# Batches of a K or V pair on separate partition halves, in a decode step of two attention and two GLU layers

## The chip, the cores and the metric

One NeuronCore of a Trainium2 chip runs the whole program. Times are device microseconds of an execution, as medians of repeated runs. PE is TensorE's matmul side, PEld its weight loads, DVE VectorE, ACT ScalarE, POOL GpSimd, SPq the queue from which the loads are issued. The profile counts sixteen DMA engines for the core, and before the change the loads fill 97.2% of their time.

## The reference

Four decode sequences of one token each go through attention, GLU, attention, GLU, each with a layer norm ahead and a residual add behind. Both attention layers use the same caches and weights, and so do both GLU layers.

```python
B, Sq, D, Hq, Hkv, Sk, Dh = 4, 1, 512, 32, 8, 8192, 128     # bf16
W = min(4096, max(256, Sk // 4))                            # window: 2048
q = (x @ wq).reshape(B, Sq, Hq, Dh).transpose(0, 2, 1, 3)
k = repeat(k_cache[:, :, Sk - W:, :], 4, axis=1)            # caches are [B, Hkv, Sk, Dh]
v = repeat(v_cache[:, :, Sk - W:, :], 4, axis=1)
p = softmax(einsum("bhqd,bhkd->bhqk", q, k) * Dh ** -0.5)
o = einsum("bhqk,bhkd->bhqd", p, v)                         # then @ wo
# GLU: (sigmoid(x @ w_gate) * (x @ w_up)) @ w_down, F = 1792
```

The windows of K and V hold 16 MiB each. K is read once and kept on the chip for the second attention layer; V is read nearly twice, 30 loads of 1 MiB, since the 25 MiB that the program sets aside (`arena`, below) do not take both whole.

## The kernel before

A small list scheduler lays out the operations of each engine from their dependencies; all loads stand in one order on the SP queue. `arena` holds 50 slots of 128 partitions x 2048 elements. A "pair" is a tile of two slots with the windows of two batches of one KV head: 2 x 512 KB = 1 MiB. One load brings it in.

```python
def pair_d(cache, h, bp):                        # the DRAM side of a K or V load
    return cache[2 * bp:2 * bp + 2, h, SK - W:SK, :].rearrange(
        "b (p j) d -> p b (j d)", p=64)          # 64 rows x 2 batches x 4096 elements

def load_k(h):
    where[("K", h)] = h
    for bp in range(2):
        dma("K%d_%d" % (h, bp), kpair(h, bp), pair_d(A_k, h, bp), w=tok(4 * h + 2 * bp), rate="bw_8k")
```

The SBUF side is a tile of 128 partitions x 4096 elements. Row p of batch b thus lands on partition 2p + b: the two batches of a pair lie interleaved over the partitions. A row is 32 tokens, 8 KB, contiguous in DRAM.

DVE transposes K (1219 ns for 128x1024 words, mean of 32 in the profile before). The program takes the result as blocks of 32 x 32 words of two bf16 elements, each transposed, so that a partition then holds some dimensions of many tokens. A score unit is 16 matmuls of 128x512, four for each of four column groups of PE. Their records overlap: 588 to 669 ns for one, and 2.00 us for the 16 of the unit at 134.49 us.

```python
for cp in range(4):
    for b in range(NB):
        gi = 2 * (b % 2) + b // 2
        kt = kpair(hk, b // 2).rearrange("p (j c x i t) -> p c t i j x", c=2, x=16, i=2, t=2)
        q0 = ((k2 * NB + b) * 4 + cp) * NR
        last = pe.matmul(ps[32 * gi:32 * gi + NR, bank, :], qbd[:, q0:q0 + NR],
                         kt[:, cp // 2, cp % 2, b % 2, :, :], start=(cp == 0), stop=(cp == 3))
```

The moving side takes x at a step of four elements (i and t lie between), because the two batches alternate. Softmax takes a row maximum on DVE and the exponential on ACT; P is then turned to stand ahead of P.V:

```python
for jh in range(2):
    for i in range(2):
        last = pe.matmul(ps[:, PBS[i], 0:256], perm[64 * i:64 * i + 64, jh * 128:(jh + 1) * 128],
                         prow[64 * i:64 * i + 64, jh * 256:(jh + 1) * 256], start=(jh == 0), stop=(jh == 1))
# ... one ACT eviction of 128x512, one DVE transpose, then 32 P.V matmuls for each pair
```

Of the kernel before, what the change touches and what calls it, by code (L numbers as in the profile page):

```python
# [6 lines left out]
F32 = mybir.dt.float32  # L7
BF16 = mybir.dt.bfloat16
ACTF = mybir.ActivationFunctionType
ALU = mybir.AluOpType  # L10
AXX = mybir.AxisListType.X
# [261 lines left out]
def build(nc, A_x, A_k, A_v, A_wq, A_wo, B_wg, B_wu, B_wd, out, cfg=None):  # L273
    cfg = dict(cfg or {})
    tm = dict(_TM)
# [8 lines left out]
    NB, SQ, D = A_x.shape  # L284
    _, HKV, SK, DH = A_k.shape
    HQ = A_wq.shape[1] // DH
    REP = HQ // HKV
    W = min(4096, max(256, SK // 4))
    NJ = W // 128
# [6 lines left out]
    NR = 4 * REP  # L296
# [18 lines left out]
    with es:  # L315
        def sb(name, shape, dt):
            return es.enter_context(nc.sbuf_tensor(name, shape, dt))

        arena = sb("arena", [128, NS * SLOT], BF16)
        prow = sb("prow", [128, 512], BF16)  # L320
        ebuf = sb("ebuf", [128, 512], F32)
        qbd = sb("qbd", [128, 2 * NB * 4 * NR], BF16)
        qh = sb("qh", [128, 2 * 64], BF16)
        qrep = sb("qrep", [128, 2 * 256], BF16)
        ones_f = sb("ones_f", [128, 32], F32)
        ident_b = sb("ident_b", [128, 128], BF16)
        perm = sb("perm", [128, 2 * 128], BF16)
        sel_f = sb("sel_f", [128, NR], F32)
        sel_b = sb("sel_b", [128, NR], BF16)
        s3 = sb("s3", [128, 2 * 3], BF16)  # L330
        sres = sb("sres", [128, 2], F32)
        sel_r = sb("sel_r", [128, REP], F32)
        maskr = sb("maskr", [128, 32], F32)
        mxt = sb("mxt", [128, 2 * 32], F32)
        nmax = sb("nmax", [128, 4], F32)
        psm = sb("psm", [128, 2], F32)
        rinv = sb("rinv", [128, 2 * NR], F32)
        onb = sb("onb", [128, 2 * NR], BF16)
# [9 lines left out]
        ps = es.enter_context(nc.psum_tensor("ps", [128, 8, 512], F32))  # L348
# [5 lines left out]
        P = _Plan()  # L354
# [3 lines left out]
        PBS = (2, 3)  # L358
# [17 lines left out]
        def c_act(n):  # L376
            return tm["act_fix"] + n * tm["act_el"]
# [43 lines left out]

        def pair_d(cache, h, bp):

            return cache[2 * bp:2 * bp + 2, h, SK - W:SK, :].rearrange("b (p j) d -> p b (j d)", p=64)

        def kpair(h, bp):
            return tile_ap(4 * h + 2 * bp)
# [81 lines left out]
        def load_v(h, bp, k, n_use):  # L509
# [6 lines left out]
                                       base=0, channel_multiplier=-1),  # L516
             r=[("ones_f",)], w=[("ident_b",)])
# [4 lines left out]

        for jh in range(2):
            for bp in range(2):
                P.op("gpsimd", "perm%d_%d" % (jh, bp), 300.0,
                     lambda g, jh=jh, bp=bp: g.affine_select(
                         perm[:, jh * 128:(jh + 1) * 128].rearrange("p (a x) -> p a x", a=4)[
                             :, :, 16 * jh + 8 * bp:16 * jh + 8 * bp + 8].rearrange("p a (i r) -> p a i r", i=2),
                         ones_f[:, :].rearrange("p (a i r) -> p a i r", a=4, i=2),
                         [[-REP, 4], [-64, 2], [-1, REP]], ALU.is_equal, 0.0,  # L530
                         base=-32 * bp, channel_multiplier=1),
                     r=[("ones_f",), ("perm",)], w=[("perm", jh, bp)])
        perms = [("perm", jh, bp) for jh in range(2) for bp in range(2)]
        P.op("vector", "sel_f", 200.0,
             lambda v: v.tensor_reduce(sel_f[:, :],
                                       perm[:, 0:128].rearrange("p (a x) -> p a x", a=4)[:, :, 0:NR].rearrange("p a x -> p x a"),
                                       AXX, ALU.add),
             r=perms, w=[("sel_f",)])
        P.op("gpsimd", "sel_b", 200.0, lambda g: g.tensor_copy(sel_b[:, :], sel_f[:, :]),
             r=[("sel_f",)], w=[("sel_b",)])  # L540
        P.op("vector", "sel_r", 100.0,
             lambda v: v.tensor_reduce(sel_r[:, :], sel_f[:, :].rearrange("p (g r) -> p r g", g=4), AXX, ALU.add),
             r=[("sel_f",)], w=[("sel_r",)])
        P.op("vector", "maskr", 100.0,
             lambda v: v.tensor_scalar(maskr[:, :].rearrange("p (y r) -> p y r", r=REP),
                                       sel_r[:, :].unsqueeze(1).broadcast_to([128, 8, REP]),
                                       1.0, 1.0e30, ALU.subtract, ALU.mult),
             r=[("sel_r",)], w=[("maskr",)])

        o = P.op("scalar", "x_in", 1300.0, lambda e: e.dma_start(x_nat, x_d), w=[("prow",)])  # L550
        o.sem = ("xin",)
# [108 lines left out]
        def q_unit(tag, h, k2):  # L660

            for a in range(4):
                dst = qbd[32 * a:32 * a + 32, k2 * 256:(k2 + 1) * 256].rearrange(
                    "p (x y) -> p x y", y=NR)[:, :, a * REP:(a + 1) * REP]
                src = qrep[32 * a:32 * a + 32, h * 64:(h + 1) * 64].rearrange("p (x r) -> p x r", r=REP)
                rd = [("qrep", h // 4)]
                if a % 2 == 0:
                    P.op("vector", "qe%s_%d" % (tag, a), c_dve(64), lambda v, dst=dst, src=src: v.tensor_copy(dst, src),  # L668
                         r=rd, w=[("q", k2, a)])
                else:  # L670
                    P.op("scalar", "qe%s_%d" % (tag, a), c_act(64), lambda s_, dst=dst, src=src: s_.copy(dst, src),  # L671
                         r=rd, w=[("q", k2, a)])
# [10 lines left out]
        def softmax_unit(tag, hk):  # L683
            u = ucount[0]
            ucount[0] += 1
            k2 = u % 2
            bank = SB[k2]
            q_unit(tag, hk, k2)

            def e_s(pe):  # L690
                last = None
                for cp in range(4):
                    for b in range(NB):
                        gi = 2 * (b % 2) + b // 2
                        kt = kpair(hk, b // 2).rearrange("p (j c x i t) -> p c t i j x", c=2, x=16, i=2, t=2)
                        q0 = ((k2 * NB + b) * 4 + cp) * NR
                        last = pe.matmul(ps[32 * gi:32 * gi + NR, bank, :], qbd[:, q0:q0 + NR],  # L697
                                         kt[:, cp // 2, cp % 2, b % 2, :, :], start=(cp == 0), stop=(cp == 3))
                return last
            P.op("tensor", "S" + tag, 16 * tm["pe_row"], e_s,  # L700
                 r=[("slot", 4 * hk + t) for t in range(4)] + [("q", k2, a) for a in range(4)],
                 w=[("pss", k2)], banks=(bank,))
            mk = mxt[:, k2 * 32:(k2 + 1) * 32]
            P.op("vector", "mx" + tag, c_dve(512),
                 lambda v: v.tensor_reduce(nmax[:, k2:k2 + 1], ps[:, bank, :], AXX, ALU.max),  # L705
                 r=[("pss", k2)], w=[("mx", k2)], banks=(bank,))
            P.op("vector", "mk" + tag, tm["dve_small"],
                 lambda v: v.tensor_scalar(mk, maskr[:, :], nmax[:, k2:k2 + 1], None, ALU.add),
                 r=[("mx", k2), ("maskr",)], w=[("mk", k2)])
            P.op("vector", "nm" + tag, tm["dve_small"],  # L710
                 lambda v: v.tensor_reduce(nmax[:, 2 + k2:3 + k2], mk, AXX, ALU.max, negate=True, apply_transpose=True),  # L711
                 r=[("mk", k2)], w=[("nm", k2)])
            P.op("scalar", "ex" + tag, c_act(512) + 200.0,
                 lambda a: a.activation(prow[:, :].rearrange("p (m x t) -> p m x t", x=16, t=2),  # L714
                                        ps[:, bank, :].rearrange("p (m t x) -> p m x t", x=16, t=2), ACTF.Exp, bias=nmax[:, 2 + k2:3 + k2], scale=1.0,
                                        accum_out=psm[:, k2:k2 + 1]),
                 r=[("pss", k2)] + [("nm", k2)], w=[("prow",), ("psm", k2)], banks=(bank,))
            return k2

        def turn_p(tag, k2):  # L720
            ob = OBS[k2]
            def e_pp(pe):
                last = None
                for jh in range(2):
                    for i in range(2):
                        last = pe.matmul(ps[:, PBS[i], 0:256], perm[64 * i:64 * i + 64, jh * 128:(jh + 1) * 128],  # L726
                                         prow[64 * i:64 * i + 64, jh * 256:(jh + 1) * 256], start=(jh == 0), stop=(jh == 1))
                return last
            P.op("tensor", "pp" + tag, tm["pe_sq"], e_pp, r=[("prow",)] + perms, w=[("ppb",)], banks=PBS)
            P.op("scalar", "pc" + tag, c_act(512),  # L730
                 lambda a: a.copy(prow[:, :].rearrange("p (y i t) -> p i y t", i=2, t=2),  # L731
                                  ps[:, PBS[0]:PBS[0] + 2, 0:256].rearrange("p i (y t) -> p i y t", t=2)),
                 r=[("ppb",)], w=[("prow",)], banks=PBS)
            P.op("vector", "pt" + tag, c_dve(256),
                 lambda v: v.transpose(ebuf[:, k2 * 256:(k2 + 1) * 256], prow[:, :].bitcast(F32)),  # L735
                 r=[("prow",)], w=[("e", k2)])
# [313 lines left out]
```

## Time and profile before

| | before |
|---|---|
| median of 4 runs (range) | 186.48 us (185.68 to 186.60) |
| profiled span | 184.4 us |
| load queue, share of sixteen DMA engines | 97.2% |
| packets of 8 KB, median duration (DMA records of the trace) | 311 ns |
| DMA packets under 512 B | 1,144 |

The first lines are from the page of the kernel before: busy time by engine; the share of the DMA engines that is busy and the rate in GB/s, in 40 equal slices of the span; the packet counts; the load queue with its packets, MB and share of sixteen engines' time; and the chain of work that ended last, by engine.

```profile
span 184.4 us, 4421 instructions
...
PE 101.2 (55%) x1944; PEld 54.7 (30%) x1944; DVE 89.5 (49%) x221; ACT 35.7 (19%) x100; POOL 14.8 (8%) x77
...
DMA  5999999999999999999999999999999999999980
GB/s 198 425 427 427 425 403 391 411 421 419 409 387 425 419 421 403 392 419 419 400 391 414 412 407 393 403 350 417 330 396 419 419 423 416 418 416 402 412 341 24
DMA packets 15379, 72.12 MB, mean 391 GB/s; under 512 B 1144, under 2 KB 5248, under 8 KB 8704
...
q1 hardware_dynamic: 15352, 71.84, 97.2%
...
DMA 52%; PE 25%; SPq 16%; DVE 4%; issue 2%; ACT 0%
```

The loads are busy in nearly every slice, in 35 of the 40 at 387 to 427 GB/s; PE and DVE are busy about half of the time. So what is saved on an engine should be hidden unless the loads get shorter; experiment 6 tests it (ratio 1.0007). The count of small packets: 71 loads with 16 completion writes each are 1,136, and the x load and the output, of 4 rows, have 4 each. That makes 1,144, so a load of 128 rows ends with 16 writes and one of 4 rows with 4. One write for each engine that worked is an inference; the DMA records bear it out, with 15 to 17 packets of 8 KB under way at once in 97.5% of the moments from 130 to 140 us.

Groups of instructions, one shape each: line, engine, operation, operands, shapes, count, then total busy us and mean ns, then idle time before them and its causes. L697 is the score matmul, L726 the turning of P, L668 and L671 copy the query into its block form.

```profile
L697 PE MATMUL ps<-arena,qbd 128*16 128x512 bf16 x256 | 32.5, 626 | 16.9 <-DVE qbd L668 8.4 <-DVE arena L678 7.5 <-issue 1.0
...
L726 PE MATMUL ps<-prow,perm 64*128 64x256 bf16 x64 | 7.4, 315 | 2.4 <-ACT prow L714 2.3
...
L668 DVE COPY qbd<-qrep 32x64 bf16<-32x64 bf16 x32 | 5.3, 166 | 0.7 <-ACT qrep L657 0.2
...
L671 ACT COPY qbd<-qrep 32x64 bf16<-32x64 bf16 x32 | 7.7, 241 | 40.9 <-PE ps L697 40.3
```

Two rows of the timeline of PE (start us, duration us, line, shape, count), in the second attention layer: the query projection, whose moving side is contiguous, and a score unit.

```profile
128.16 1.02 PE L626 MATMUL ps<-arena,xn 128*4 128x512 bf16 x8
...
134.49 2.00 PE L697 MATMUL ps<-arena,qbd 128*16 128x512 bf16 x16 [0.16 <-DVE qbd L668]
```

```profile
126.69 17.58 SPq L382 DMA_DIRECT2D arena<-in_A_v_cache_dram  x14
```

### The profile page before, as it was taken

Reading aid. Unit: us, or ns where it says so; the run is one execution under the profiler, and the core shown is the slowest. Engines: PE = TensorE matmul, PEld = TensorE weight load, DVE = VectorE, ACT = ScalarE, POOL = GpSimd, SP = SyncE. Lnnn points to the kernel's source line nnn. Section 1 sums busy time; section 2 is a strip of 40 time slices with the busy share of each in tenths; the row PEclk is TensorE's granted clock in tenths of the full one; section 3 lists DMA queues with packets and bytes.
Section 4 is the critical chain, followed back from the end, with each engine's and each line's share of the span. In section 5 each row is a group of like instructions: output and inputs, shape, how many; then the busy total and the mean of one; then the engine's idle time right before and its main releaser. Section 6 shows DMA issues by size and latency. Waiting matters only on the chain.

```text
span 184.4 us, 4421 instructions
## 1 busy us (share of the span) xinstructions
PE 101.2 (55%) x1944; PEld 54.7 (30%) x1944; DVE 89.5 (49%) x221; ACT 35.7 (19%) x100; POOL 14.8 (8%) x77
## 2 busy tenths in 40 slices
PE   0532423652807327173373545445979997994474
PEld 0101000332303323023232441210334653584422
DVE  5209998477592565925621531138463442340330
ACT  2003022240212103011020001001365442220010
POOL 4000000110000101010010000000022111120000
PEclk9999995585766756755555555555897897885569
DMA  5999999999999999999999999999999999999980
GB/s 198 425 427 427 425 403 391 411 421 419 409 387 425 419 421 403 392 419 419 400 391 414 412 407 393 403 350 417 330 396 419 419 423 416 418 416 402 412 341 24
DMA packets 15379, 72.12 MB, mean 391 GB/s; under 512 B 1144, under 2 KB 5248, under 8 KB 8704
## 3 DMA queue, kind: packets, MB, share of 16 engines
q1 hardware_dynamic: 15352, 71.84, 97.2%
q8 instruction: 15, 0.25, 0.5%
q14 instruction: 4, 0.03, 0.0%
q10 hardware_dynamic: 8, 0.00, 0.0%
HBM read 71.83 MB, written 0.00 MB: 390 GB/s over the span
## 4 chain that ended last, share of the span: by engine, by line
DMA 52%; PE 25%; SPq 16%; DVE 4%; issue 2%; ACT 0%
DMA arena<-in_A_v_cache_dram 33%; SPq L382 16%; PE ps L697 11%; DMA arena<-in_B_w_down_dram 9%; PE ps L770 8%; DMA arena<-in_A_wq_dram 5%; DMA arena<-in_B_w_up_dram 5%; PE ps L726 2%; PE ps L794 1%; DVE ps L492 1%; PE ps L626 1%; DVE nmax L705 1%; PE ps L749 1%; PE ps L905 1%; PE ps L852 1%
## 5 line engine op out<-in xcount | busy, mean ns | idle before, releaser
L770 PE MATMUL ps<-ebuf,arena 128*128 128x8 bf16 x1024 | 31.0, 167 | 29.7 <-DMA arena<-in_A_v_cache_dram 22.1
L697 PE MATMUL ps<-arena,qbd 128*16 128x512 bf16 x256 | 32.5, 626 | 16.9 <-DVE qbd L668 8.4
L770 PEld LDWEIGHTS ps<-ebuf,arena 128*128 128x128 bf16 x1024 | 28.8, 101 | 36.3 <-DMA arena<-in_A_v_cache_dram 32.5
L678 DVE STREAM_TRANSPOSE arena<-arena 128x1024 f32<-128x1024 f32 x32 | 37.9, 1219 | 3.3 <-DMA arena<-in_A_k_cache_dram 3.0
L705 DVE TENSOR_REDUCE nmax<-ps 128x1 f32<-128x512 f32 x16 | 11.0, 687 | 26.0 <-PE ps L697 26.0
L714 ACT ACTIVATE prow<-ps,nmax 128x512 bf16<-128x512 f32 x16 | 11.0, 687 | 39.6 <-DVE nmax L711 24.9
L671 ACT COPY qbd<-qrep 32x64 bf16<-32x64 bf16 x32 | 7.7, 241 | 40.9 <-PE ps L697 40.3
L697 PEld LDWEIGHTS ps<-arena,qbd 128*16 128x16 bf16 x256 | 6.1, 97 | 31.3 <-issue 22.0
L739 POOL CAST s<-psm 128x1 bf16<-128x1 f32 x16 | 3.0, 188 | 144.4 <-ACT prow L714 144.4
L778 DVE TENSOR_TENSOR onb<-ps,rinv 128x16 bf16<-128x16 f32 x16 | 2.9, 184 | 21.1 <-PE ps L770 21.1
L626 PE MATMUL ps<-arena,xn 128*4 128x512 bf16 x64 | 7.8, 582 | 7.6 <-DMA arena<-in_A_wq_dram 6.2
L794 PE MATMUL ps<-onb,arena 128*128 128x4 bf16 x256 | 9.1, 166 | 3.1 <-DVE onb L778 3.1
L731 ACT CAST prow<-ps 128x512 bf16<-128x512 f32 x16 | 9.4, 587 | 7.1 <-PE ps L726 7.0
L735 DVE STREAM_TRANSPOSE ebuf<-prow 128x256 f32<-128x256 f32 x16 | 7.0, 437 | 6.7 <-ACT prow L731 6.4
L852 PE MATMUL ps<-arena,xn 128*4 128x448 bf16 x64 | 6.5, 560 | 4.9 <-DVE xn L607 3.1
L794 PEld LDWEIGHTS ps<-onb,arena 128*128 128x128 bf16 x256 | 7.9, 101 | 4.1 <-DVE onb L778 2.8
L726 PE MATMUL ps<-prow,perm 64*128 64x256 bf16 x64 | 7.4, 315 | 2.4 <-ACT prow L714 2.3
L596 ACT ACTIVATE lnv<-lnv 128x4 f32<-128x4 f32 x4 | 0.8, 205 | 34.0 <-DVE lnv L593 34.0
L634 DVE STREAM_TRANSPOSE ebuf<-ps 128x512 f32<-128x512 f32 x4 | 2.9, 715 | 7.7 <-PE ps L626 7.6
L859 DVE STREAM_TRANSPOSE ebuf<-ps 128x448 f32<-128x448 f32 x4 | 2.6, 650 | 7.8 <-PE ps L852 7.8
L668 DVE COPY qbd<-qrep 32x64 bf16<-32x64 bf16 x32 | 5.3, 166 | 0.7 <-ACT qrep L657 0.2
L749 PE MATMUL ps<-sel_b,s 128*128 128x16 bf16 x48 | 3.8, 175 | 3.2 <-POOL s L743 2.4
(61 smaller groups left out, 68.1 us busy)
## 6 DMA issues: line engine op xcount, KB each, us to landing
arena<-in_A_v_cache_dram SPq DMA_DIRECT2D x30, 1024.0 KB, 16.8
arena<-in_A_k_cache_dram SPq DMA_DIRECT2D x16, 1024.0 KB, 16.0
arena<-in_A_wq_dram SPq DMA_DIRECT2D x8, 1024.0 KB, 9.4
arena<-in_A_wo_dram SPq DMA_DIRECT2D x4, 1024.0 KB, 24.3
arena<-in_B_w_gate_dram SPq DMA_DIRECT2D x4, 896.0 KB, 19.7
arena<-in_B_w_up_dram SPq DMA_DIRECT2D x4, 896.0 KB, 15.8
arena<-in_B_w_down_dram SPq DMA_DIRECT2D x2, 1024.0 KB, 12.5
arena<-in_B_w_down_dram SPq DMA_DIRECT2D x1, 768.0 KB, 7.0
```

What stands on the lines that cost most here:

```text
L382: o = P.op("sync", name, 0.0, lambda e, dst=dst, src=src: e.dma_start(dst, src), r=r, w=w, dma_bytes=nbytes, dma_rate=tm[rate])
L626: last = pe.matmul(ps[32 * hh:32 * hh + NB, qb, :], xn[:, c * NB:(c + 1) * NB], tile_ap(s)[:, o + hh * 512:o + (hh + 1) * 512], start=(c = ...
L671: P.op("scalar", "qe%s_%d" % (tag, a), c_act(64), lambda s_, dst=dst, src=src: s_.copy(dst, src), r=rd, w=[("q", k2, a)])
L678: P.op("vector", "T%d_%d" % (h, t), c_dve(1024), lambda v, v32=v32: v.transpose(v32, v32), r=[("slot", 4 * h + t)], w=[("slot", 4 * h + t)])
L697: last = pe.matmul(ps[32 * gi:32 * gi + NR, bank, :], qbd[:, q0:q0 + NR], kt[:, cp // 2, cp % 2, b % 2, :, :], start=(cp == 0), stop=(cp = ...
L705: lambda v: v.tensor_reduce(nmax[:, k2:k2 + 1], ps[:, bank, :], AXX, ALU.max),
L714: lambda a: a.activation(prow[:, :].rearrange("p (m x t) -> p m x t", x=16, t=2), ps[:, bank, :].rearrange("p (m t x) -> p m x t", x=16, t ...
L726: last = pe.matmul(ps[:, PBS[i], 0:256], perm[64 * i:64 * i + 64, jh * 128:(jh + 1) * 128], prow[64 * i:64 * i + 64, jh * 256:(jh + 1) * 2 ...
L731: lambda a: a.copy(prow[:, :].rearrange("p (y i t) -> p i y t", i=2, t=2), ps[:, PBS[0]:PBS[0] + 2, 0:256].rearrange("p i (y t) -> p i y t ...
L770: last = pe.matmul(ps[:, ob, bp * 8:bp * 8 + 8], src[:, j * 128:(j + 1) * 128], ev[:, j % 2, j % 16 // 2, x0:x0 + 8], start=(j == 0), stop ...
L794: last = pe.matmul(ps[:, WB, c * NB:(c + 1) * NB], tile_ap(s)[:, o + r_ * D + c * 128:o + r_ * D + (c + 1) * 128], ov[:, r_ * NB:(r_ + 1) ...
L852: last = pe.matmul(ps[32 * g:32 * g + NB, OBS[n], 0:NF], xn[:, c * NB:(c + 1) * NB], tile_ap(s)[:, o:o + NF], start=(c == 0), stop=(c == N ...
```

## The change

The two batches are to lie on separate halves of the partitions: batch 0 of a pair on partitions 0 to 63, batch 1 on 64 to 127. Then a 32-wide block of transposed K holds one batch alone, the score matmul takes both halves of a row block at a step of two elements in place of four, the query block needs half of its columns, and one 128x512 matmul turns P. In exchange the row maximum of a head lies on two partition halves, so two more DVE copies bring them together.

The diff, cut to its core:

```diff
         def pair_d(cache, h, bp):
-            return cache[2 * bp:2 * bp + 2, h, SK - W:SK, :].rearrange("b (p j) d -> p b (j d)", p=64)
+            return cache[2 * bp:2 * bp + 2, h, SK - W:SK, :].rearrange("b (p j) d -> b p (j d)", p=64)
 ...
-                    for b in range(NB):
-                        gi = 2 * (b % 2) + b // 2
-                        kt = kpair(hk, b // 2).rearrange("p (j c x i t) -> p c t i j x", c=2, x=16, i=2, t=2)
-                        q0 = ((k2 * NB + b) * 4 + cp) * NR
+                    for gi in range(4):
+                        jh, bp = gi // 2, gi % 2
+                        kt = kpair(hk, bp).rearrange("p (j c x t) -> p c t j x", c=2, x=32, t=2)
+                        q0 = ((k2 * 2 + bp) * 4 + cp) * NR
                         last = pe.matmul(ps[32 * gi:32 * gi + NR, bank, :], qbd[:, q0:q0 + NR],
-                                         kt[:, cp // 2, cp % 2, b % 2, :, :], start=(cp == 0), stop=(cp == 3))
+                                         kt[:, cp // 2, cp % 2, jh * NJ:(jh + 1) * NJ, :], start=(cp == 0), stop=(cp == 3))
 ...
+            for g in range(2):
+                P.op("vector", "nx%d%s" % (g, tag), tm["dve_small"],
+                     lambda v, g=g: v.tensor_copy(nmax[64 * g:64 * g + 64, 4 + k2:5 + k2],
+                                                  nmax[64 - 64 * g:128 - 64 * g, k2:k2 + 1]), ...)
 ...
-            def e_pp(pe):          # four matmuls of 64x256
-                ...
+            P.op("tensor", "pp" + tag, tm["pe_sq"],
+                 lambda pe: pe.matmul(ps[:, PBS[0], :], perm[:, :], prow[:, :], start=True, stop=True), ...)
```

Left out: the smaller `qbd`, the masks and the permutation for the new order, and the views of the exponential and of the eviction. Order, bytes and row size of the loads do not change.

More of the change, by code (lines that the diff above doesn't have):

```diff
@@ L321, in build @@
         ebuf = sb("ebuf", [128, 512], F32)
-        qbd = sb("qbd", [128, 2 * NB * 4 * NR], BF16)
+        qbd = sb("qbd", [128, 2 * 2 * 4 * NR], BF16)
         qh = sb("qh", [128, 2 * 64], BF16)
@@ L326, in build @@
         ident_b = sb("ident_b", [128, 128], BF16)
-        perm = sb("perm", [128, 2 * 128], BF16)
+        perm = sb("perm", [128, 128], BF16)
         sel_f = sb("sel_f", [128, NR], F32)
@@ L331, in build @@
         sres = sb("sres", [128, 2], F32)
-        sel_r = sb("sel_r", [128, REP], F32)
+        sel_r = sb("sel_r", [128, 2 * REP], F32)
         maskr = sb("maskr", [128, 32], F32)
         mxt = sb("mxt", [128, 2 * 32], F32)
-        nmax = sb("nmax", [128, 4], F32)
+        nmax = sb("nmax", [128, 6], F32)
         psm = sb("psm", [128, 2], F32)
@@ L524, in build @@
             for bp in range(2):
-                P.op("gpsimd", "perm%d_%d" % (jh, bp), 300.0,
-                     lambda g, jh=jh, bp=bp: g.affine_select(
-                         perm[:, jh * 128:(jh + 1) * 128].rearrange("p (a x) -> p a x", a=4)[
-                             :, :, 16 * jh + 8 * bp:16 * jh + 8 * bp + 8].rearrange("p a (i r) -> p a i r", i=2),
-                         ones_f[:, :].rearrange("p (a i r) -> p a i r", a=4, i=2),
-                         [[-REP, 4], [-64, 2], [-1, REP]], ALU.is_equal, 0.0,
-                         base=-32 * bp, channel_multiplier=1),
-                     r=[("ones_f",), ("perm",)], w=[("perm", jh, bp)])
-        perms = [("perm", jh, bp) for jh in range(2) for bp in range(2)]
+                for i in range(2):
+                    z0 = 16 * jh + 8 * bp + REP * i
+                    P.op("gpsimd", "perm%d_%d_%d" % (jh, bp, i), 200.0,
+                         lambda g, jh=jh, bp=bp, i=i, z0=z0: g.affine_select(
+                             perm[:, 64 * i:64 * i + 64].rearrange("p (y z) -> p y z", y=2)[:, :, z0:z0 + REP],
+                             ones_f[:, 0:2 * REP].rearrange("p (y r) -> p y r", y=2),
+                             [[-REP, 2], [-1, REP]], ALU.is_equal, 0.0,
+                             base=-(64 * jh + 32 * bp + 2 * REP * i), channel_multiplier=1),
+                         r=[("ones_f",), ("perm",)], w=[("perm", jh, bp, i)])
+        perms = [("perm", jh, bp, i) for jh in range(2) for bp in range(2) for i in range(2)]
         P.op("vector", "sel_f", 200.0,
-             lambda v: v.tensor_reduce(sel_f[:, :],
-                                       perm[:, 0:128].rearrange("p (a x) -> p a x", a=4)[:, :, 0:NR].rearrange("p a x -> p x a"),
-                                       AXX, ALU.add),
+             lambda v: v.tensor_reduce(sel_f[:, :], perm[:, :].rearrange("p (g x) -> p x g", x=NR), AXX, ALU.add),
              r=perms, w=[("sel_f",)])
@@ L541, in build @@
         P.op("vector", "sel_r", 100.0,
-             lambda v: v.tensor_reduce(sel_r[:, :], sel_f[:, :].rearrange("p (g r) -> p r g", g=4), AXX, ALU.add),
+             lambda v: v.tensor_reduce(sel_r[:, :], sel_f[:, :].rearrange("p (g y) -> p y g", g=2), AXX, ALU.add),
              r=[("sel_f",)], w=[("sel_r",)])
-        P.op("vector", "maskr", 100.0,
-             lambda v: v.tensor_scalar(maskr[:, :].rearrange("p (y r) -> p y r", r=REP),
-                                       sel_r[:, :].unsqueeze(1).broadcast_to([128, 8, REP]),
-                                       1.0, 1.0e30, ALU.subtract, ALU.mult),
-             r=[("sel_r",)], w=[("maskr",)])
+        P.op("vector", "maskr_z", 100.0, lambda v: v.memset(maskr[:, 16:32], 1.0e30), w=[("maskr_z",)])
+        for i in range(2):
+            P.op("vector", "maskr%d" % i, 100.0,
+                 lambda v, i=i: v.tensor_scalar(maskr[:, 8 * i:8 * i + 8].rearrange("p (y r) -> p y r", r=REP),
+                                                sel_r[:, REP * i:REP * i + REP].unsqueeze(1).broadcast_to([128, 2, REP]),
+                                                1.0, 1.0e30, ALU.subtract, ALU.mult),
+                 r=[("sel_r",)], w=[("maskr", i)])
         o = P.op("scalar", "x_in", 1300.0, lambda e: e.dma_start(x_nat, x_d), w=[("prow",)])
@@ L662, in q_unit @@
             for a in range(4):
-                dst = qbd[32 * a:32 * a + 32, k2 * 256:(k2 + 1) * 256].rearrange(
-                    "p (x y) -> p x y", y=NR)[:, :, a * REP:(a + 1) * REP]
-                src = qrep[32 * a:32 * a + 32, h * 64:(h + 1) * 64].rearrange("p (x r) -> p x r", r=REP)
+                dst = qbd[32 * a:32 * a + 32, k2 * 128:(k2 + 1) * 128].rearrange(
+                    "p (l c y) -> p l c y", l=2, y=NR)[:, :, :, a * REP:(a + 1) * REP]
+                src = qrep[32 * a:32 * a + 32, h * 64:(h + 1) * 64].rearrange(
+                    "p (l i c r) -> p i l c r", l=2, i=2, r=REP)[:, a // 2]
                 rd = [("qrep", h // 4)]
@@ L706, in softmax_unit @@
                  r=[("pss", k2)], w=[("mx", k2)], banks=(bank,))
+            for g in range(2):
+                P.op("vector", "nx%d%s" % (g, tag), tm["dve_small"],
+                     lambda v, g=g: v.tensor_copy(nmax[64 * g:64 * g + 64, 4 + k2:5 + k2],
+                                                  nmax[64 - 64 * g:128 - 64 * g, k2:k2 + 1]),
+                     r=[("mx", k2)], w=[("nx", k2, g)])
             P.op("vector", "mk" + tag, tm["dve_small"],
-                 lambda v: v.tensor_scalar(mk, maskr[:, :], nmax[:, k2:k2 + 1], None, ALU.add),
-                 r=[("mx", k2), ("maskr",)], w=[("mk", k2)])
+                 lambda v: v.scalar_tensor_tensor(mk, nmax[:, 4 + k2:5 + k2].broadcast_to([128, 32]), nmax[:, k2:k2 + 1],
+                                                  maskr[:, :], ALU.max, ALU.add),
+                 r=[("mx", k2), ("nx", k2, 0), ("nx", k2, 1), ("maskr", 0), ("maskr", 1), ("maskr_z",)], w=[("mk", k2)])
             P.op("vector", "nm" + tag, tm["dve_small"],
@@ L713, in softmax_unit @@
             P.op("scalar", "ex" + tag, c_act(512) + 200.0,
-                 lambda a: a.activation(prow[:, :].rearrange("p (m x t) -> p m x t", x=16, t=2),
-                                        ps[:, bank, :].rearrange("p (m t x) -> p m x t", x=16, t=2), ACTF.Exp, bias=nmax[:, 2 + k2:3 + k2], scale=1.0,
+                 lambda a: a.activation(prow[:, :].rearrange("p (m x t) -> p m x t", x=32, t=2),
+                                        ps[:, bank, :].rearrange("p (m t x) -> p m x t", x=32, t=2), ACTF.Exp, bias=nmax[:, 2 + k2:3 + k2], scale=1.0,
                                         accum_out=psm[:, k2:k2 + 1]),
@@ L721, in turn_p @@
             ob = OBS[k2]
-            def e_pp(pe):
-                last = None
-                for jh in range(2):
-                    for i in range(2):
-                        last = pe.matmul(ps[:, PBS[i], 0:256], perm[64 * i:64 * i + 64, jh * 128:(jh + 1) * 128],
-                                         prow[64 * i:64 * i + 64, jh * 256:(jh + 1) * 256], start=(jh == 0), stop=(jh == 1))
-                return last
-            P.op("tensor", "pp" + tag, tm["pe_sq"], e_pp, r=[("prow",)] + perms, w=[("ppb",)], banks=PBS)
-            P.op("scalar", "pc" + tag, c_act(512),
-                 lambda a: a.copy(prow[:, :].rearrange("p (y i t) -> p i y t", i=2, t=2),
-                                  ps[:, PBS[0]:PBS[0] + 2, 0:256].rearrange("p i (y t) -> p i y t", t=2)),
-                 r=[("ppb",)], w=[("prow",)], banks=PBS)
+            P.op("tensor", "pp" + tag, tm["pe_sq"],
+                 lambda pe: pe.matmul(ps[:, PBS[0], :], perm[:, :], prow[:, :], start=True, stop=True),
+                 r=[("prow",)] + perms, w=[("ppb",)], banks=(PBS[0],))
+            P.op("scalar", "pc" + tag, c_act(512), lambda a: a.copy(prow[:, :], ps[:, PBS[0], :]),
+                 r=[("ppb",)], w=[("prow",)], banks=(PBS[0],))
             P.op("vector", "pt" + tag, c_dve(256),
```

## The prediction

> **What bounds the kernel now.** The loads. The page gives the load queue 97.2% of sixteen DMA engines' span, 72.12 MB, mean 391 GB/s, up to 427 in a slice; the chain of waits is 52% DMA and 16% load issue. PE is 55% busy, DVE 49%. The DMA records hold 6,667 packets of 8 KB, median 311 ns: 26.3 GB/s for one engine.
>
> **What the change does to compute (small, under the loads).**
> - Score matmuls: step 4 to step 2 elements. The timeline shows 16 of them (128x512, four column groups) in 2.0 us, 0.50 us per four; the query projection, with step 1, takes 1.02 us for 8, 0.51 per four. So step 4 costs nothing and step 2 saves nothing.
> - P turned by one 128x512 matmul instead of four 64x256 (0.39 to 0.61 us a unit): about even. The 587 ns eviction behind it keeps its size.
> - Query copies halve from 64 to 32 elements (DVE 166, ACT 241 ns each): perhaps 30 ns off, an estimate from the small DVE operations (162 to 175 ns).
> - Two more one-column DVE copies per unit, about 0.16 us each by those operations: 0.3 us on the softmax chain, 16 times, under the loads.
>
> Alone: within 1%.
>
> **What it does to the loads (large).** K and V come in 46 loads of 1 MiB (16 K, 30 V). Before, a load's DRAM side counts 64 rows, then 2 batches, then 4096 elements; after, 2 batches, then 64 rows. The SBUF side is 128 partitions in both. Order, bytes and 8 KB rows stay. But the slowest dimension of the source falls from 64 to 2.[...] The trace of before agrees where it can: 1,144 packets are under 512 B, which is 71 loads x 16 completions plus 4 each for the x load and the output, both of 4 rows. No load in it has 2 on one side: the decisive case is untested.
>
> **Sum.** On two engines a K or V load is 64 packets x 311 ns = 19.9 us per engine; 46 of them 916 us. They also carry their sixteenth of the weights: from packet medians about 59 us (wq 20, wo 12, gate and up 18, down 9). That is 975 us[...]. Start 2 us, tail after the last landing 3 us, gaps at the layer change a few us.
>
> **Predicted: 980 us**, 8 in 10 within 950 to 1010. Chances: faster by over 2% 0.04, within 2% 0.06, slower 0.90.
>
> **What would show it.** Right: K and V landings about 20 us apart; packets under 512 B fall by 46 x 14 = 644 to 500; load queue near 18% of sixteen engines' span, mean about 74 GB/s; the chain of waits almost wholly DMA; the score matmuls stay near 2 us a unit.
>
> **What would make it wrong.** If the split follows the 128 partitions of the SBUF side, or the source is regrouped, the loads stay near 420 GB/s and the time is 185 to 188 us. If a lone engine moves 8 KB much faster or slower than 311 ns, the size is off.

Two engines: no trace in hand showed it, so two was the assumption, to be tested. 916 and 59 us are 975 us, with start, tail and gaps about 980. Start and tail are of the trace of before: its load queue moves its first packet 1.84 us after the start of the span, and its last load is complete at 181.3 of 184.4 us.

## More of the kernel before

Who waited for whom (us in total, times, longest): P.V for a load of V. Below it, the load queue's timeline: the 14 loads of V of the second layer were issued in 17.58 us.

```profile
PE ps L770 <- DMA arena<-in_A_v_cache_dram: 22.1, 11, 5.5
```

## The result, and the profile after

The changed kernel takes 994.22 us (993.16 to 995.62, 4 runs) against 186.48 us: ratio 5.3352, 95% interval 5.3183 to 5.3520. A ratio here is the mean time of one kernel's fast runs over that of the other's of the same rounds, so it is not quite the ratio of the medians quoted. A run counts as slow when it is over 1.5% above the fastest of its kernel; the others are the fast ones.

The same lines of the page, of the kernel after:

```profile
span 991.6 us, 4363 instructions
...
PE 103.6 (10%) x1896; PEld 56.1 (6%) x1896; DVE 96.4 (10%) x255; ACT 34.9 (4%) x100; POOL 14.7 (1%) x81
...
DMA  4111211111121111131111211256111111111243
GB/s 195 53 54 54 87 53 53 53 53 54 68 71 54 53 53 54 54 87 53 53 54 53 86 52 54 82 142 263 54 54 53 54 53 54 53 54 53 83 127 122
DMA packets 14735, 72.12 MB, mean 73 GB/s; under 512 B 500, under 2 KB 4604, under 8 KB 8060
...
q1 hardware_dynamic: 14708, 71.83, 19.6%
...
another core or an unknown queue 44%; DMA 26%; SPq 22%; PE 5%; issue 0%; DVE 0%; ACT 0%; POOL 0%
```

In 27 of the 40 slices the rate is 53 or 54 GB/s, with little over a tenth of the DMA engines' time busy: what two engines of sixteen move at 26 to 27 GB/s each. Small packets fell by 644 to 500, exactly 46 loads times 14 completions. Slices at 87, 142 or 263 GB/s are ones in which weights move. The chain of waits is a trap: it books 44% to "another core or an unknown queue", though the program runs on one core and all of its large loads are on one queue. The table of waits names the releaser:

```profile
PE ps L771 <- DMA arena<-in_A_v_cache_dram: 693.4, 30, 58.7
```

P.V waits 693.4 us for loads of V, before 22.1 us. The groups that answer to those of before (L711 are the new copies), then PE's timeline for P.V of the second layer, and the load queue's row for the V loads of that layer:

```profile
L699 PE MATMUL ps<-arena,qbd 128*16 128x512 bf16 x256 | 29.2, 601 | 157.5 <-DVE arena L680 80.3 <-DVE qbd L670 77.2
...
L731 PE MATMUL ps<-prow,perm 128*128 128x512 bf16 x16 | 9.1, 570 | 3.6 <-ACT prow L722 3.6
...
L670 DVE COPY qbd<-qrep 32x32 bf16<-32x32 bf16 x32 | 5.2, 162 | 0.9 <-ACT qrep L658 0.2
...
L673 ACT COPY qbd<-qrep 32x32 bf16<-32x32 bf16 x32 | 6.9, 215 | 251.3 <-PE ps L699 250.7
...
L711 DVE COPY nmax<-nmax 64x1 f32<-64x1 f32 x32 | 4.7, 147 | 1.0
```

```profile
752.23 1.02 PE L771 MATMUL ps<-ebuf,arena 128*128 128x8 bf16 x32 [15.82 <-DMA arena<-in_A_v_cache_dram]
771.93 1.02 PE L771 MATMUL ps<-ebuf,arena 128*128 128x8 bf16 x32 [18.68 <-DMA arena<-in_A_v_cache_dram]
...
791.62 1.01 PE L771 MATMUL ps<-ebuf,arena 128*128 128x8 bf16 x32 [15.82 <-DMA arena<-in_A_v_cache_dram]
811.31 1.01 PE L771 MATMUL ps<-ebuf,arena 128*128 128x8 bf16 x32 [18.68 <-DMA arena<-in_A_v_cache_dram]
```

```profile
689.14 235.38 SPq L382 DMA_DIRECT2D arena<-in_A_v_cache_dram  x14
```

P.V starts every 19.7 us (752.23, 771.93, 791.62, 811.31), one V load each. Sixty-four packets of 309 ns, the median of 8 KB packets in this trace, are 19.8 us. The compute side did what was said of it and it is of no weight: the turning of P is 9.1 us in place of 7.4 us busy, and the two new copies are 147 ns each.

### The profile page after: what moved, and what is told of

It reads as the page before. It is cut to its first block, busy times and chain, and to the rows that moved or that the text cites. A ratio compares the mean times of both kernels' runs of the same rounds, so it can differ in the third digit from the quotient of the medians.

```text
span 991.6 us, 4363 instructions
## 1 busy us (share of the span) xinstructions
PE 103.6 (10%) x1896; PEld 56.1 (6%) x1896; DVE 96.4 (10%) x255; ACT 34.9 (4%) x100; POOL 14.7 (1%) x81
## 3 DMA queue, kind: packets, MB, share of 16 engines
q1 hardware_dynamic: 14708, 71.83, 19.6%
## 4 chain that ended last, share of the span: by engine, by line
another core or an unknown queue 44%; DMA 26%; SPq 22%; PE 5%; issue 0%; DVE 0%; ACT 0%; POOL 0%
DMA arena<-in_A_v_cache_dram 23%; SPq L382 22%; DMA arena<-in_B_w_down_dram 3%; PE ps L771 2%; PE ps L699 1%; DMA arena<-in_A_wq_dram 1%; PE ps L795 0%; PE ps L906 0%; ACT prow L722 0%; PE ps L731 0%; PE ps L750 0%; DVE onb L779 0%; PE ps L627 0%; PE ps L930 0%
## 5 line engine op out<-in xcount | busy, mean ns | idle before, releaser
L771 PE MATMUL ps<-ebuf,arena 128*128 128x8 bf16 x1024 | 32.4, 168 | 693.4 <-DMA arena<-in_A_v_cache_dram 693.4
L699 PE MATMUL ps<-arena,qbd 128*16 128x512 bf16 x256 | 29.2, 601 | 157.5 <-DVE arena L680 80.3
L673 ACT COPY qbd<-qrep 32x32 bf16<-32x32 bf16 x32 | 6.9, 215 | 251.3 <-PE ps L699 250.7
L731 PE MATMUL ps<-prow,perm 128*128 128x512 bf16 x16 | 9.1, 570 | 3.6 <-ACT prow L722 3.6
L757 DVE RECIPROCAL rinv<-ps 128x16 f32<-128x16 f32 x16 | 3.8, 240 | 34.5 <-PE ps L750 34.3
L670 DVE COPY qbd<-qrep 32x32 bf16<-32x32 bf16 x32 | 5.2, 162 | 0.9 <-ACT qrep L658 0.2
L711 DVE COPY nmax<-nmax 64x1 f32<-64x1 f32 x32 | 4.7, 147 | 1.0
L492 DVE STREAM_TRANSPOSE ps<-arena 128x512 f32<-128x512 f32 x4 | 2.5, 696 | 19.9 <-DMA arena<-in_A_v_cache_dram 19.9
```

Source lines behind the costliest of these rows:

```text
L673: P.op("scalar", "qe%s_%d" % (tag, a), c_act(64), lambda s_, dst=dst, src=src: s_.copy(dst, src), r=rd, w=[("q", k2, a)])
L731: lambda pe: pe.matmul(ps[:, PBS[0], :], perm[:, :], prow[:, :], start=True, stop=True),
L771: last = pe.matmul(ps[:, ob, bp * 8:bp * 8 + 8], src[:, j * 128:(j + 1) * 128], ev[:, j % 2, j % 16 // 2, x0:x0 + 8], start=(j == 0), stop ...
```

## The experiments

Theory A: the loads of K and V run on two engines, because the slowest dimension of their source is now 2, and that is all of the loss. Rivals: B, the compute side's new waits cost part of it; C, all engines work, but rows far apart in DRAM are slow. D and E came up on the way. Every run below passed the comparison with the reference, also those with a wrong layout, so that comparison tells nothing of the layout here. The runs of experiments 1, 2, 3 and 5 have one time each; nothing under several per cent is read from them.

### 1. The load's order alone, in the kernel before

```diff
 # the kernel before
-            ... .rearrange("b (p j) d -> p b (j d)", p=64)
+            ... .rearrange("b (p j) d -> b p (j d)", p=64)
```

> The kernel before with one edit: the source of the K and V loads walked batch by batch (2 x 64 rows) in place of row by row (64 x 2). Batches then land on the wrong partitions, so the result is wrong on purpose; every compute instruction is that of the kernel before. Theory A[...]: 985 to 1000 us, packets under 512 B 500, all of the loss from this one edit. Theory B (the compute side of the change, its new waits, costs a noticeable part of the 808 us): clearly under 980 us.

Measured: 995.95 us. Its page, with rates and packets:

```profile
span 994.2 us, 4421 instructions
...
DMA  4111211111211111121111211256111111111243
GB/s 195 53 53 53 87 53 53 54 53 53 73 66 54 53 53 53 54 87 51 53 54 53 88 51 53 82 138 261 55 53 53 54 54 53 54 53 54 82 129 117
DMA packets 14736, 72.12 MB, mean 73 GB/s; under 512 B 501, under 2 KB 4605, under 8 KB 8061
```

501 small packets, one off the count of 500, and 53 GB/s. One edit to the load gives the whole loss with the compute of before. B falls.

### 2. The two halves near each other

```diff
 # the kernel after
-            return cache[2 * bp:2 * bp + 2, h, SK - W:SK, :].rearrange("b (p j) d -> b p (j d)", p=64)
+            return cache[2 * bp, h].rearrange("(c q) d -> c q d", c=2)[:, 0:2048, :].rearrange("c (p j) d -> c p (j d)", p=64)
```

> The changed kernel with loads of 2 x 64 rows again, but both halves out of one batch, 1 MiB apart in place of 16 MiB (wrong result on purpose). Theory A (two engines because of the 2): unchanged, 985 to 1000 us. Theory C (all engines work, but reads 16 MiB apart get in each other's way in DRAM): much faster, below 800 us.

Measured: 994.97 us. With 1 MiB between the halves in place of 16 MiB nothing changes; C falls as the cause of the 994 us.

### 3. Four, eight and sixteen in the slowest place

The same bytes and rows, other counts in front (wrong layouts):

```diff
 # k4: 4 batches x 32 rows
+            return cache[0:4, h, SK - W + 1024 * bp:SK - W + 1024 * bp + 1024, :].rearrange("b (p j) d -> b p (j d)", p=32)
 # k8: 8 heads x 16 rows (t0 here and below: a start token that differs from load to load)
+            return cache[2 * bp + h // 4, 0:8, t0:t0 + 512, :].rearrange("g (p j) d -> g p (j d)", p=16)
 # far16: 2 batches x 8 heads = 16 slabs x 8 rows
+            return cache[2 * bp:2 * bp + 2, 0:8, t0:t0 + 256, :].rearrange("b g (p j) d -> (b g) p (j d)", p=8)
```

> The changed kernel with K and V loads of 4 batches x 32 rows (1 MiB of 8 KB rows as before, batches still 16 MiB apart, wrong result on purpose). Theory A: 4 engines, 32 packets of 309 ns each on them a load, 46 x 32 x 0.309 = 455 us, plus what the rest took in the two known runs (184.4 - 114 = 70 with 16 engines, 991.6 - 910 = 82 with 2), so 525 to 540 us; packets under 512 B 1144 - 46 x 12 = 592. Theory C: no faster than the changed kernel, about 990 us, since it has twice the streams at the same distance.

> The changed kernel with K and V loads of 8 heads x 16 rows, heads 2 MiB apart (wrong result on purpose). Theory A: 8 engines, 46 x 16 x 0.309 = 227 us plus 70 to 82 us for the rest: 297 to 312 us; packets under 512 B 1144 - 46 x 8 = 776.

> The changed kernel with K and V loads of 16 slabs (2 batches x 8 heads, 2 MiB apart) x 8 rows, the slabs in the slowest place (wrong result on purpose; 1 MiB of 8 KB rows, as before). Theory A: [...]16 engines and 184 to 190 us, packets under 512 B 1144. Theory C (it is the distance of the rows, or the walk by slabs, that is slow): well over 200 us.

| slowest dimension | time, us | theory A expected | small packets | 8 KB packets: median, mean ns |
|---|---|---|---|---|
| 2 (after) | 994.22 | | 500 | 309, 321 |
| 4 | 551.13 | 525 to 540 | 592 | 309, 330 |
| 8 | 364.68 | 297 to 312 | 776 | 314, 385 |
| 16 (16 slabs) | 275.55 | 184 to 190 | 1,144 | 547, 523 |
| 64 (before) | 186.48 | | 1,144 | 311, 319 |

The packet counts are exactly those of 4, 8 and 16 engines, so the number of engines is as theory A has it. The DMA records show as much: in a stretch in which K and V stream alone, the number of 8 KB packets under way at once is 2 in the changed kernel (98% of the moments from 740 to 930 us), 4 with four in front (95%, 400 to 460 us) and 8 with eight (91%, 280 to 320 us). The times are not as it has them: they miss by 11, 53 and 86 us over the upper end, and the packets got longer. The page of the 16 slabs:

```profile
span 273.8 us, 4348 instructions
...
DMA  7999999999999999999999999999999999999992
GB/s 271 399 233 231 231 235 271 236 232 232 233 235 240 236 237 236 241 255 244 248 250 234 265 241 238 399 396 363 325 233 236 239 249 261 258 275 261 323 416 98
DMA packets 15379, 72.12 MB, mean 263 GB/s; under 512 B 1144, under 2 KB 5248, under 8 KB 8704
```

The DMA engines are busy in nearly every slice and yet move some 230 to 240 GB/s in most of those in which K and V stream. A second cost had been overlooked.

### 4. The correct layout on sixteen engines, by two loads a pair

Each pair is loaded by two loads, each of one batch and 64 partitions, 64 rows on both sides. The result is correct in layout.

```diff
 # the kernel after, in dma(): a K or V load becomes two, one semaphore takes both
+        def halves(dst, src):
+            return [(dst[64 * b:64 * b + 64, :], src[b]) for b in range(2)]
```

The control is the kernel before with its loads cut into two of 64 partitions likewise (32 rows x 2 batches each):

```diff
+            return [(dst[64 * b:64 * b + 64, :], src[32 * b:32 * b + 32]) for b in range(2)]
```

> The changed kernel, correct, with each K or V load cut into two of one batch and 64 partitions (64 rows of 8 KB on both sides[...]). All compute of the change stays. Theory A: 16 engines, 92 loads in place of 46, packets under 512 B 1144 + 46 x 16 = 1880, and the time is that of the kernel before within 1.5%: 184 to 189 us, since the loads bound both. Theory D (a load that writes only half of the partitions cannot run at the full rate, so that the layout itself costs): 220 us or more.

> Control: the kernel before with each K or V load cut into two of 64 partitions (32 rows x 2 batches each, correct). Theory A: 16 engines, 185 to 189 us; what it costs over the kernel before is the price of twice the loads, to be taken off the run with the change's compute. Theory D: 220 us or more, like the changed kernel with halves.

Measured in 5 rounds: the changed kernel with halves 286.85 us median (6 runs; the two fast 281.48 and 284.34), ratio to before 1.5212 (1.5107 to 1.5317); the control 291.23 us median (7 runs; fast ones 285.93 and 288.78), ratio 1.5451 (1.5345 to 1.5557). Many runs of both were over 1.5% above their fastest. The page of the changed kernel with halves (this profile is of a run of 285.97 us):

```profile
span 284.2 us, 4409 instructions
...
DMA  7999999999999999999999999999999999999991
GB/s 277 386 220 220 216 223 262 221 220 221 220 228 246 221 219 221 220 244 222 221 220 219 241 229 227 304 368 353 416 231 234 239 250 278 278 276 274 338 400 45
DMA packets 16116, 72.13 MB, mean 254 GB/s; under 512 B 1880, under 2 KB 5984, under 8 KB 9440
```

Small packets are 1,880 as expected: sixteen engines. But the rate is 220 GB/s and the median 8 KB packet 588 ns, near twice 309. Theory A's time fails here and D's holds, for the control as well (285.93 and 288.78 us in its fast runs). So it isn't the compute of the change: loads that write 64 partitions each ran at about half of the rate, 220 in place of some 420 GB/s. By what means is not shown. Loads of half the size that write all 128 partitions were not run, so a cost of twice as many loads is not excluded by a run; but the time is in the packets themselves and not in gaps between loads: sixteen under way at 588 ns each are 223 GB/s, about the rate measured, and in every slice but the first and the last the DMA engines are busy for 90% or more.

### 5. Rows of a slab or distance: thirty-two slabs of four rows

Theory E: with sixteen engines at work, the second loss hangs on how many neighbouring partitions a slab fills, 8 in the run with 16 slabs, and not on where the slabs lie in DRAM. Thirty-two slabs of four rows fill 4 partitions each, with slabs as far apart as in the 16-slab run and twice as many.

```diff
 # the kernel after, wrong layout on purpose
+            return cache[0:4, 0:8, t0:t0 + 128, :].rearrange("b g (p j) d -> (b g) p (j d)", p=4)
```

> The changed kernel with K and V loads of 32 slabs (4 batches x 8 heads, 2 MiB apart) x 4 rows (wrong result on purpose; 1 MiB of 8 KB rows on 128 partitions, as in the run with 16 slabs x 8 rows, which took 275.55 us with half of its 8 KB packets at 547 ns). Theory E[...]: 184 to 190 us and 8 KB packets back at a median of 309 to 315 ns. Theory C (the loss is the walk by slabs or their distance in DRAM): 260 us or more, since slabs are as far apart and twice as many.

Measured: 185.64 us; 8 KB packets back at a median of 311 ns.

```profile
span 183.8 us, 4348 instructions
...
DMA  5999999999999999999999999999999999999980
GB/s 193 424 426 428 422 404 387 414 426 421 404 389 424 414 421 413 384 424 422 401 385 422 406 408 392 411 340 416 371 406 419 424 419 419 426 412 400 411 342 19
DMA packets 15379, 72.12 MB, mean 392 GB/s; under 512 B 1144, under 2 KB 5248, under 8 KB 8704
```

Distance and the walk by slabs cost nothing (185.64 us against 185.92 us for before), and C falls for the second loss too. The two runs differ by 90 us, in the number of slabs and in how many neighbouring partitions a slab fills, so E is supported. The trace does not say which engine wrote which partition, so why slabs of 8 rows had packets of 547 ns and slabs of 4 rows of 311 ns is not shown. The misses with four and eight engines were not taken apart; with four, the 8 KB packets from 400 to 460 us average 311 ns, so that miss arose in other stretches.

### 6. The compute side with loads as fast as before

```diff
 # the kernel after, result wrong on purpose: batches interleaved, compute takes them as halves
-            ... .rearrange("b (p j) d -> b p (j d)", p=64)
+            ... .rearrange("b (p j) d -> p b (j d)", p=64)
```

> The changed kernel with the source order of the K and V loads put back (64 rows x 2 batches), so that they run on 16 engines and write all partitions as before. Batches then lie interleaved while the compute takes them as halves, so the result is wrong on purpose; every compute instruction and wait is that of the change. It shows what the compute side of the change is worth when the loads are as fast as before. Theory A (the loads bound it; the compute side moves nothing): 184 to 188 us, within 1% of before. If the score matmuls at step 2 are worth something: under 184 us, and score matmuls of attention 2 clearly under the 1.9 us a unit of before.

Measured in 5 rounds: 185.95 us (184.95 to 187.05, 6 runs) against 185.92 us; ratio 1.0007 (0.9967 to 1.0046). At equal load speed the change is worth nothing that can be measured. Yet three score units of the second layer were short; PE's timeline, then the score group:

```profile
130.63 1.10 PE L699 MATMUL ps<-arena,qbd 128*16 128x512 bf16 x16
...
134.46 1.08 PE L699 MATMUL ps<-arena,qbd 128*16 128x512 bf16 x16 [2.08 <-DVE nmax L719]
...
143.92 1.88 PE L699 MATMUL ps<-arena,qbd 128*16 128x512 bf16 x16 [0.17 <-issue]
```

```profile
L699 PE MATMUL ps<-arena,qbd 128*16 128x512 bf16 x256 | 27.8, 577 | 21.5 <-DVE qbd L670 8.9 <-DVE arena L680 6.4 <-ACT prow L722 3.9
```

The group is 27.8 us busy in place of 32.5 us, so the prediction's "step 2 saves nothing" is in doubt. Two last runs change the moving read alone.

### 7. The step of the moving read

```diff
 # the kernel of experiment 6; step4:
-                        kt = kpair(hk, bp).rearrange("p (j c x t) -> p c t j x", c=2, x=32, t=2)
+                        kt = kpair(hk, bp).rearrange("p (j c x i t) -> p c t i j x", c=2, x=16, i=2, t=2)
 # step1, contiguous:
+                        kt = kpair(hk, bp).rearrange("p (n m) -> p n m", m=512)
```

> The changed compute with fast loads (the run before it but one, 185.95 us), with only the moving read of the score matmuls put back to a step of four elements (wrong result on purpose). Theory F (the step alone sets a score matmul's rate where the granted clock is full: in that run 1.08 us a unit of 16 at clock 1.00, in the kernel before 1.91 us at clock 1.00): every unit back to 1.9 to 2.0 us, also at full clock. Theory G (the shorter units came from something else, as the smaller query tile or the order of the batches): units of about 1.1 us at full clock stay. In both the whole takes 184.5 to 188 us, since the loads bound it.

> The same with the moving read contiguous, step one (wrong result on purpose). Theory F[...]: no further gain, units of 1.05 to 1.12 us at full clock[...]. The whole 184.5 to 188 us.

Measured in 3 rounds: step 4 186.95 us, ratio 1.0062 (1.0015 to 1.0109); step 1 186.32 us, ratio 1.0032 (0.9977 to 1.0087). A score unit at step 4, then two at step 1:

```profile
131.39 2.01 PE L699 MATMUL ps<-arena,qbd 128*16 128x512 bf16 x16
```

```profile
131.28 1.32 PE L699 MATMUL ps<-arena,qbd 128*16 128x512 bf16 x16
...
140.42 1.88 PE L699 MATMUL ps<-arena,qbd 128*16 128x512 bf16 x16
```

The clock of these units, from tables of stretches: start and end, length, busy us and count of PE, PEld, DVE, ACT and POOL, then the recorded clock of PE as a share of full speed (the third number from the end), the DMA share and GB/s. The first row is that unit at step 4, the others are two of the step-2 units of experiment 6 above.

```profile
131.39:133.30 1.91, 1.91 (x33) 0.58 (x27) 1.82 (x7) 0.22 (x2) 0.00 (x0) 1.00 0.87 326
```

```profile
130.63:131.70 1.07, 1.07 (x20) 0.34 (x12) 1.07 (x3) 0.23 (x2) 0.00 (x0) 1.00 0.94 337
...
143.92:145.70 1.78, 1.78 (x16) 0.38 (x16) 0.51 (x2) 0.59 (x1) 0.24 (x2) 0.50 1.02 428
```

Over whole programs the picture is plain. At step 4 (before, its controls, step4) every unit of 16 takes about 2.0 us (1.93 to 2.09), whether its clock is recorded as 1.00 or as 0.50; only two units with an idle gap in them took longer (3.49 and 4.32 us). (The 1.91 us that an expectation above gives for before is the length of the stretch; the unit took 2.00.) At step 2, over all runs, each of the 13 units that lie wholly at a recorded 1.00 takes 1.04 to 1.13 us, and each that lies wholly at 0.50 takes 1.88 us. In the units of 1.32 to 1.66 us the record begins or changes on the way and the matmuls change with it: at 131.28 us of step1 a matmul takes 634 ns at first, and about 380 ns once the record of 1.00 has begun at 131.86 us. Step 4 thus caps the rate at full clock, F holds, and G falls. One thing came along with the step: at step 4 the innermost run of the read is 16 elements long, at step 2 it is 32, and no run separates the two.

No unit of the contiguous read lies wholly at 1.00, so its shortest (1.32 us) can't be set against 1.08. Within units it can: at 1.00 a set of four matmuls, one for each column group, starts 217 or 219 ns after the set before it at step 1, 215 to 240 at step 2 and 412 to 472 at step 4. So no loss of step 2 against step 1 is to be seen.

A word of caution on the clock. These traces have no record of it before the first change, and the page counts such a stretch as full: the first record stands at 130.2 us in the run of experiment 6 and at 281.5 of 284.2 us in the run with halves. The mean of 0.997 that is given for the latter thus says nothing of its score units, which took 1.88 to 1.92 us, like units recorded at 0.50. Why the clock was at 0.50 or at 1.00 in a stretch is not shown.

## Why the prediction was right

- **The step that decided: two engines.** Right. Experiment 1 gives all of the loss by the load alone, experiment 2 excludes the distance, and the small packets follow the slowest dimension of the source in every run: 500 with 2, 592 with 4, 776 with 8, 1,144 with 16, 32 and 64. Other counts than these powers of two were not run, and the SBUF side had 128 partitions in all of these, so the runs give no wider rule.
- **19.9 us a load.** 19.7 us measured, from the starts of P.V.
- **The sum.** 980 us predicted, 994.22 us measured, inside 950 to 1010. The mis-sized term is "They also carry their sixteenth of the weights: from packet medians about 59 us". The load queue's 19.6% of sixteen engines over 991.6 us is 194 us an engine; less K and V (5,888 packets x 309 ns / 16 = 114 us), 80 us are left. The same subtraction for before, 97.2% of 184.4 us less 114.5 us, gives 65 us. So some 6 us of the miss are medians used where means were needed (in K and V as in the weights), and 15 us are packets that grew: those of 3,584 B from 144 to 212 ns on average, those of 1 KB from 50 to 71 ns. The 8 KB packets grew beside the weights as well: with the span after the change cut into 40 slices, they average 310 to 311 ns in the slices without weight packets (the first, of 329 ns, apart) and 318 to 394 ns in those with over 200 of them. K and V were 10 us less (46 x 19.7 = 906 in place of 916), which makes up for part. So weights and K and V slow each other; by what means was not tested, and the mean over all engines need not be that of the two.
- **"If the split follows the 128 partitions of the SBUF side."** It doesn't (500 small packets): that case did not arise.
- **Compute within 1%.** Right: 1.0007. Of its terms, the copies on DVE 147 ns (0.16 us said), the ACT query copies 241 to 215 ns (30 ns off said), those on DVE only 166 to 162 ns, the turning of P 0.57 us a unit against 0.46 us (9.1 and 7.4 us for 16; "about even" was said).
- **"Step 4 costs nothing and step 2 saves nothing."** Wrong in itself, without effect on the time. The projection that it was compared with had the same 0.5 us for four matmuls, but it stood in a stretch with a recorded clock of 0.50, and the score unit at 134.49 us in one with 1.00. Equal times at half and at full clock meant that the score unit, at full clock, lost half of its rate to its read (2.00 us at step 4 against 1.04 to 1.13 us at step 2). Step 2 saved 4.7 us of PE's busy time (32.5 to 27.8), all under the loads.
- **What the prediction did not see.** That two engines were only the first of two obstacles: also on sixteen engines the layout that the change wants was filled at about half of the rate (220 in place of some 420 GB/s) by loads of one batch each. It bears on the remedy, not on the number.

The one correct version of the new layout on sixteen engines (experiment 4) is slower than before, by half. Nor is there much to find: with loads as fast as before, its compute side changes nothing. Not tried in any run: two load queues working on opposite halves at once.

## What to carry to other kernels

When a load's pattern is rewritten, look at the slowest dimension of its DRAM side before anything else: a 2 in front of 64 rows put 46 loads on two engines and turned 186 us into 994 us, and the count of small packets (1,144 to 500) shows it at once. After that look at which partitions are written at one time, for a layout that fills one half of the partitions after the other here ran at 220 in place of some 420 GB/s even with all engines at work. And ask first whether the engine that is to be relieved bounds the kernel: here it did not.
